# Short token tails of an expert layer: fp32 products of unsplit w2, four k at once in 32 array columns each

## The chip, the cores and the metric

The kernel runs on one core of a Trainium2 chip. The metric is device time in microseconds of one execution; the kernel before has a median of 837.87 us over three runs (837.8 to 838.12). The engines are TensorE (PE, with PEld for its weight loads), VectorE (DVE), ScalarE (ACT), GpSimd (POOL) and SyncE (SP), which here only issues DMA transfers. Each has an instruction queue of its own and runs it in order; semaphores tie them together.

## What is computed

Block-causal attention over 8 batches, 8 heads, 576 tokens and 64 dimensions makes 4608 rows of 512. Each row then goes to one of 16 experts (four groups of four), chosen by the largest logit, and its result is scaled by the two softmax weights:

```python
for g in range(G):
    mask_g = g_idx == g
    ...
    for e in range(Eg):
        mask_e = e_idx == e
        ...
        h = np.maximum(xg[mask_e] @ w1[g, e], 0.0)      # 512 -> 1024
        ye = h @ w2[g, e]                               # 1024 -> 512
        combined = g_w[mask_g][mask_e] * e_w[mask_e]
        out[tok_idx] = combined[:, None] * ye
```

## The kernel before

The first half of the span is attention, with the router among it. This case is about the second half, class `Moe`. Tokens are dealt into 15 **slots**, each one expert's tokens or part of them. The first ("e") has 512 tokens of the expert that is fullest after six batches; the others have fixed sizes, `CAPS` in units of 16 tokens, run in the order `EXEC`. In that order the slots have 528, 144, 448, 144, 448, 192, 416, 256, 320, 256, 320, 288, 272 and 128 tokens. In names a slot has its place in `CAPS`: `y6` belongs to the slot of 288 tokens, `h7` to the one of 272.

A slot's tokens are gathered (POOL, indirect DMA), transposed (`xt`, line 925) and put through two products. `g1` makes h = relu(x w1): the 1024 hidden units are eight k of 128, each four matmuls deep. `g2` makes y += h w2, with h as the stationary operand and 512 columns of w2 streaming. Precision comes from splitting: every fp32 operand becomes a high part in fp32r and the remainder (low), and three products (high high, low high, high low) stand for one fp32 product. Slots under 256 tokens leave w1 unsplit and multiply in fp32 (line 952), the others take the split (line 957). The relu of `g1` is made twice: ScalarE writes the high part (line 970), VectorE the low one (line 974).

Whole chunks of 128 tokens take three matmuls per k in `g2` (line 1002). What lies beyond them, when it is at most 64 tokens, is the **tail**. It puts its high and low part side by side into the stationary operand, `gap` columns apart (32 for up to 32 tokens, else 64), so that wh and wl each stream once: two matmuls per k (line 1007). The store (lines 1013 to 1035) then adds the two halves: a scaled copy of the low half on ScalarE (line 1020), and on VectorE the high half times the weight plus that copy (line 1021). Whole chunks are scaled by VectorE or ScalarE alone (lines 1027, 1029). GpSimd writes the rows out.

Weights come in **units** of 512 KB, eight per slot: w1 and w2 in turn, each for two k. SP loads a unit into one of four `raw` buffers; ScalarE casts it to wh, VectorE subtracts to wl, in two pieces each (lines 908, 909). There are `WBUFS` = 9 pairs of wh and wl. Unsplit w1 goes straight into a wh buffer (line 900).

The order of the work is written out beforehand. `plan` makes one list of steps: `g1` of k 0, the last `g2` of the slot before, `g1` of k 1, `g2` of k 0, and so on (a step is one k; two where the slot has 144 to 256 tokens, four where it has 128). It adds up TensorE's time by step and gives each weight piece a due time 9 us ahead of its first use (14 us for unsplit w1). `run` issues the steps; after each it issues transposes, loads (`pump`), the pieces that are due, at most two unless more are needed (`advance`), index loads (`getids`) and gathers, all into the queues of their engines. A piece may only be issued when the unit that had its buffer `WBUFS` units earlier has been used up (`limit`).

The router's logits (line 673) and the products of the attention weights with V (line 304) serve the prediction as measures. Both are fp32 and use a part of the array's columns:

```python
nc.tensor.matmul(ps[32 * c:32 * c + 32, z, 0:288], lhsT=self.w[p, c, :], rhs=xT[p, c, ks],     # L673, p: 64 rows
                 start=True, stop=True, tile_position=(64 * z, 32 * c))
...
    for a in range(2):
        nc.tensor.matmul(                                                                      # L304, 128 rows
            o[64 * a:64 * a + 64, hf, c0:c0 + BLK * (b1 - t)], lhsT=r["v"][:, a, j, :],
            rhs=pt[:, PTJ * j + t:PTJ * j + b1, a, :],
            start=x == 0, stop=x == len(pcs) - 1, tile_position=(0, 64 * a),
        )
```

A matmul in fp32 has two records in the trace, one in fp32r has one.

Of the kernel before, what the change touches and what calls it, by code (L numbers as in the profile page):

```python
# [8 lines left out]
F32 = mybir.dt.float32  # L9
# [3 lines left out]
AF = mybir.ActivationFunctionType  # L13
ALU = mybir.AluOpType
# [3 lines left out]
P = 128  # L18
D = 64
S = 576  # L20
# [372 lines left out]
CAPS = [33, 28, 28, 26, 20, 20, 18, 17, 16, 16, 12, 9, 9, 8]  # L393
EXEC = [0, 12, 1, 11, 2, 10, 3, 9, 4, 8, 5, 6, 7, 13]
EBAT = 6
WBUFS = 9
XBUFS = 5
PIECE = 760.0
LEAD = 9000.0
# [410 lines left out]
class Moe:  # L810
# [17 lines left out]
    def grow(self):  # L828
        t = self.at.vfix.tile([P, 6 * NT * D], F32R, tag="vb", name="hx")
        self.ring.append(t[:, 0:1152])  # L830

    def hbuf(self):
        self.nring += 1
        return self.ring[(self.nring - 1) % len(self.ring)]

    def slot(self, n, m, row, idx):
        T = UNIT * m
        nf, r = divmod(T, P)
        ch = [(c, P) for c in range(nf)] + ([(nf, r)] if r else [])
        nk = 1 if T > 256 else min(8, 1 << (512 // T).bit_length() - 1)  # L840
        return dict(n=n, m=m, T=T, gap=32 if r <= 32 else 64, nf=nf + (r > 64), tail=r if r <= 64 else 0, ch=ch, row=row, idx=idx, u={}, x={},
                    small=T < 256, nk=nk, nb=8 // nk)

    def index(self, s):
# [3 lines left out]
    def getids(self, s):  # L848
        if "ids" in s:
            return  # L850
        nc = self.nc
        s["st"] = nc.sync.value_load(s["row"][0:1, s["idx"], 1:2], min_val=0, max_val=PADS)
        s["ids"] = ids = self.ip.tile([P, 5, 2], I32, tag="ids", name=f"ids{s['n']}")
        table = lambda o, n: self.ro.tab[bass.ds(s["st"] + o, n), 0:2]
        full = s["T"] // P
        todo = [(ids[:, 0:full, :], table(0, full * P).rearrange("(c p) t -> p c t", p=P))] if full else []
        r = s["T"] % P
        if r:
            todo += [(ids[z:z + r, full, :], table(full * P, r)) for z in ((0, s["gap"]) if s["tail"] else (0,))]
        for o, i in todo:  # L860
            self.ro.after_writes(nc.sync.dma_start(o, i))

# [72 lines left out]
    def g1(self, s, b):  # L935
        nc = self.nc
        nk, T, r = s["nk"], s["T"], s["tail"]
        n = nk * T
        w0 = n if n <= 512 else n // 2
        ps = []  # L940
        for a in range(0, n, w0):
            p = self.at.psH(f"h{s['n']}_{b}_{a}")[:, 0:w0]
            ps.append((a, p))
            tw = min(T, w0)
            for k in range(w0 // tw):
                kg = b * nk + k
                w = self.w(s, 2 * (kg // 2))
                f = slice(kg % 2 * P, kg % 2 * P + P)
                o, t = p[:, k * tw:(k + 1) * tw], slice(a, a + tw)
                for dc in range(4):  # L950
                    if s["small"]:
                        nc.tensor.matmul(o, lhsT=w[0][:, dc, f].bitcast(F32), rhs=s["xh"][:, dc, t].bitcast(F32),  # L952
                                         start=dc == 0, stop=dc == 3)
                        continue
                    wh, wl = w
                    for x, (ww, rr) in enumerate(((wh, s["xh"]), (wh, s["xl"]), (wl, s["xh"]))):
                        nc.tensor.matmul(o, lhsT=ww[:, dc, f], rhs=rr[:, dc, t],  # L957
                                         start=dc == 0 and x == 0, stop=dc == 3 and x == 2)
        buf = self.hbuf()
        F = T - r  # L960
        pad = s["gap"] - r if r else 0
        L = T + pad
        g = buf[:, 0:nk * (L + T)].rearrange("p (k t) -> p k t", k=nk)
        hi, lt, lf = g[:, :, 0:T], g[:, :, L:L + r], g[:, :, L + r:L + T]
        if pad:
            nc.gpsimd.memset(g[:, :, T:L].bitcast(F32), 0.0)
        for a, p in ps:
            wa = min(T, w0)
            pv = p.rearrange("p (k t) -> p k t", t=wa)
            nc.scalar.activation(hi[:, :, a:a + wa], pv, AF.Relu)  # L970
            for t, t0, t1 in ((lf, 0, F), (lt, F, T)):
                q0, q1 = max(a, t0), min(a + wa, t1)
                if q0 < q1:
                    nc.vector.scalar_tensor_tensor(out=t[:, :, q0 - t0:q1 - t0], in0=pv[:, :, q0 - a:q1 - a], scalar=0.0,  # L974
                                                   in1=hi[:, :, q0:q1].bitcast(F32), op0=ALU.max, op1=ALU.subtract)
        s["h", b] = (hi, lf, g[:, :, F:L + r])

# [10 lines left out]
    def g2(self, s, b):  # L988
        nc = self.nc
        nk, T = s["nk"], s["T"]  # L990
        if b == 0:
            self.ytile(s)
        y, ks = s["y"], range(b * nk, (b + 1) * nk)

        for c in range(s["nf"]):
            n = s["ch"][c][1]
            r = slice(c * P, c * P + n)
            for k in ks:
                h, l = [t[:, k % nk, r] for t in s["h", b][0:2]]
                wh, wl = [w[:, k % 2, :] for w in self.w(s, 2 * (k // 2) + 1)]  # L1000
                for x, (hh, w) in enumerate(((h, wh), (h, wl), (l, wh))):
                    nc.tensor.matmul(y[c][0:n], lhsT=hh, rhs=w, start=k == 0 and x == 0, stop=k == 7 and x == 2)  # L1002
        if s["tail"]:
            n = s["gap"] + s["tail"]
            for k in ks:
                for x, w in enumerate(self.w(s, 2 * (k // 2) + 1)):
                    nc.tensor.matmul(y[s["nf"]][0:n], lhsT=s["h", b][2][:, k % nk, :], rhs=w[:, k % 2, :],  # L1007
                                     start=k == 0 and x == 0, stop=k == 7 and x == 1)
        if b == s["nb"] - 1:
            for c in range(len(s["ch"])):  # L1010
                self.store(s, c, c < s["nf"])

    def store(self, s, c, full):
        nc = self.nc
        ys = self.ro.rows.tile([P, 512], F32, tag="row", name=f"ys{s['n']}_{c}")
        n, y, cw = s["ch"][c][1], s["y"][c], s["ids"][:, c, 1:2].bitcast(F32)
        if not full:
            tmp = self.ro.rows.tile([P, 512], F32, tag="row", name=f"yt{s['n']}")
            z = s["gap"]
            nc.scalar.activation(tmp[0:n], y[z:z + n], AF.Copy, scale=cw[z:z + n])  # L1020
            nc.vector.scalar_tensor_tensor(out=ys[0:n], in0=y[0:n], scalar=cw[0:n], in1=tmp[0:n],
                                           op0=ALU.mult, op1=ALU.add)
        elif s.get("o") == len(self.slots) - 1:
            nc.scalar.activation(ys[0:n, 0:256], y[0:n, 0:256], AF.Copy, scale=cw[0:n])  # L1024
            nc.vector.tensor_scalar(out=ys[0:n, 256:512], in0=y[0:n, 256:512], scalar1=cw[0:n], scalar2=None, op0=ALU.mult)
        elif c % 2 == 0:
            nc.vector.tensor_scalar(out=ys[0:n], in0=y[0:n], scalar1=cw[0:n], scalar2=None, op0=ALU.mult)  # L1027
        else:
            nc.scalar.activation(ys[0:n], y[0:n], AF.Copy, scale=cw[0:n])
        nc.gpsimd.memset(self.ro.mark, 0.0)  # L1030
        i = nc.gpsimd.indirect_dma_start(  # L1031
            out=self.out, out_offset=bass.IndirectOffsetOnAxis(ap=s["ids"][0:n, c, 0:1], axis=0),
            in_=ys[0:n], in_offset=None, bounds_check=NTOK - 1, oob_is_err=False)
        self.ro.apart("out", i)

    def plan(self, slots):
        self.slots = slots
        seq = []
# [11 lines left out]
            prev = (s, "g2", s["nb"] - 1)  # L1050
        seq.append(prev)
        self.seq = seq
        self.units = [(s, u) for s in slots for u in range(8)]
        self.first, self.last = {}, {}
        self.tc0, t = [], 0.0
        self.begin = {}
        for n, (s, f, b) in enumerate(seq):
            self.tc0.append(t)
            nk = s["nk"]
            if f == "g1":  # L1060
                t += nk * 4 * s["T"] * (4 if s["small"] else 3) / 2.4
            else:
                t += nk * (3 * s["nf"] + 2 * (s["tail"] > 0)) * 216
            if (f, b) == ("g1", 0):
                self.begin[s["o"]] = n
                t += 430.0 * len(s["ch"])
            for k in range(b * nk, (b + 1) * nk):
                key = (s["o"], 2 * (k // 2) + (f == "g2"))
                self.first.setdefault(key, n)
                self.last[key] = n  # L1070
# [7 lines left out]
        for p in range(len(self.pieces) - 1, -1, -1):  # L1078
            ui, s, u, z = self.pieces[p]
# [54 lines left out]
    def run(self, hooks):  # L1134
        total = len(self.seq)
        for n, (s, f, b) in enumerate(self.seq):
# [3 lines left out]
            ready = n >= FREE  # L1140
# [11 lines left out]
            if ready:  # L1152
                for x in self.slots[1:]:
                    if "ids" not in x and self.tc0[self.begin[x["o"]]] - now < ILEAD:
                        self.getids(x)
            self.gathers(now, ready)
            yield

    def overflow(self, cnti, row):
# [19 lines left out]
def attention_moe(ctx, tc, q, k, v, w_group, w_expert, w1, w2, out, order=None, on_dve=None):  # L1179
    nc = tc.nc  # L1180
# [15 lines left out]
    with tc.manual_schedule(engines={ET.PE, ET.Activation, ET.DVE, ET.Pool, ET.SP}):  # L1196
        ro = Router(tc, ctx, consts, w_group, w_expert, tab, xd)
        moe = Moe(tc, ctx, consts, ro, w1, w2, out)
# [64 lines left out]
        for j in range(1, 3):  # L1263
            b("X", j)
        at.experts()
        b("G", 0)
        b("G", 1)
        for _ in run:
# [28 lines left out]
```

## Time and profile before

| | |
|---|---|
| median of the runs | 837.87 us |
| profiled execution: its time | 836.7 us |
| its span | 835.0 us |
| TensorE, VectorE, ScalarE, GpSimd busy | 95%, 63%, 60%, 32% |
| DMA in the whole span | 126.67 MB, 152 GB/s |
| raw weight loads | 96 of 512 KB |

The span is what the profiler saw between the first and the last instruction; the execution's own time is 1.7 us longer. Busy time is how long an engine had an instruction in it. Matmuls overlap, so a record is longer than the time until the next one starts; what a matmul costs is read from start to start, or from the chain. The chain is the work that ended last, followed back from the end: a line's share of it is what the span would lose without it, as long as nothing else becomes late.

### The profile page before, as it was taken

What the parts mean: (1) busy time and instruction counts of PE and PEld (TensorE: products, weight loads), DVE (VectorE), ACT (ScalarE), POOL (GpSimd) and SP (SyncE); (2) the same over time, 40 slices, a digit from 0 to 9 for tenths busy, and PEclk for the clock granted to TensorE, in tenths of its full rate; (3) what the DMA queues carried; (4) which work ended last, traced back from release to release, by engine and by line L of the source; (5) the groups of instructions that cost most, each with busy time, mean ns of one, the idle gap of its engine ahead of it and who ended that gap; (6) DMA issues with size and microseconds to landing.
All of it is one profiled execution on the core that took longest, in us unless ns stands there. A gap on an engine that the chain in (4) does not pass through costs nothing.

```text
span 835.0 us, 20289 instructions
## 1 busy us (share of the span) xinstructions
PE 795.5 (95%) x7649; PEld 649.7 (78%) x7649; DVE 529.3 (63%) x1102; ACT 504.6 (60%) x1273; POOL 265.9 (32%) x444
## 2 busy tenths in 40 slices
PE   8899999999999999879999999999999999999996
PEld 4677777777777777657888888888988989888885
DVE  4566989898989898668353544554444655655552
ACT  4899999999999998742342433433344445545541
POOL 3563344444444345443232211221221221131101
PEclk9899999999999999999999999999999999999999
DMA  7466473626363633641555736645544666575471
GB/s 153 114 185 181 109 157 78 155 71 150 83 152 78 145 84 90 198 153 36 177 166 162 236 117 205 201 133 192 197 145 148 203 207 191 179 237 177 151 236 39
DMA packets 182258, 126.67 MB, mean 152 GB/s; under 512 B 124902, under 2 KB 156214, under 8 KB 182160
## 3 DMA queue, kind: packets, MB, share of 16 engines
q1 hardware_dynamic: 173072, 100.73, 43.4%
q0 software_dynamic: 9088, 24.64, 8.6%
q8 instruction: 61, 1.00, 0.6%
q14 instruction: 37, 0.30, 0.1%
HBM read 100.88 MB, written 24.59 MB: 150 GB/s over the span
## 4 chain that ended last, share of the span: by engine, by line
PE 54%; DVE 1%; issue 0%; POOLq 0%; ACT 0%; ACTq 0%
PE y L1002 20%; PE h L957 19%; PE y L1007 5%; PE h L952 4%; PE ye L1002 2%; PE xp L925 2%; PE he L957 2%; POOLq L1293 0%; DVE gsc L712 0%; DVE gdd L710 0%; DVE goh L714 0%; DVE pre L742 0%; PE spill L612 0%; ACT ys L1024 0%; DVE sel L724 0%
## 5 line engine op out<-in xcount | busy, mean ns | idle before, releaser
L242 ACT ACTIVATE pb<-s,nm 128x512 f32<-128x512 f32 (+4 forms) x288 | 156.7, 556 | 31.3 <-DVE nm L230 26.7
L957 PE MATMUL h<-xt,wh 128*128 128x264 f32 (+6 forms) x704 | 155.3, 312 | 0.0
L909 DVE TENSOR_TENSOR wl<-raw,wh 128x512 fp32r<-128x512 f32 x192 | 123.4, 685 | 11.2 <-ACT wh L908 10.6
L230 DVE TENSOR_REDUCE nm<-s 128x2 f32<-128x1024 f32 (+4 forms) x160 | 122.9, 801 | 11.1 <-PE s L225 5.8
L957 PEld LDWEIGHTS h<-xt,wh 128*128 128x128 f32 x704 | 119.3, 188 | 9.1
L908 ACT CAST wh<-raw 128x512 fp32r<-128x512 f32 x192 | 108.8, 620 | 2.0 <-DMA raw<-in_moe_w_dram 1.7
L957 PE MATMUL h<-xt,wl 128*128 128x264 f32 (+6 forms) x352 | 109.3, 311 | 0.0
L1002 PE MATMUL y<-wh,hring 128*128 128x512 f32 x306 | 107.2, 401 | 0.0
L221 PE MATMUL s<-qk 64*128 64x512 f32 (+3 forms) x768 | 90.8, 351 | 12.6 <-ACT pb L242 7.3
L275 ACT COPY pt<-tp 128x1024 f32<-128x1024 f32 (+4 forms) x160 | 100.8, 747 | 0.5 <-PE tp L150 0.5
L1031 POOL DMA_INDIRECT out_dram<-ys,ids x40 | 41.2, 1029 | 183.4 <-DVE ys L1027 170.0
L970 ACT ACTIVATE hring<-h 128x288 fp32r<-128x288 f32 (+7 forms) x62 | 28.9, 466 | 114.0 <-PE h L957 55.3
L974 DVE SCALAR_TENSOR_TENSOR hring<-h,hring 128x32 fp32r<-128x32 f32 (+7 forms) x112 | 35.7, 357 | 97.5 <-ACT hring L970 89.2
L304 PE MATMUL o<-pt,vb 128*64 128x320 f32 (+4 forms) x896 | 93.9, 360 | 1.1 <-issue 1.1
L187 POOL CAST qk<-nf 128x640 fp32r<-128x640 f32 (+1 forms) x63 | 43.0, 694 | 150.8 <-ACT nf L275 140.4
L304 PEld LDWEIGHTS o<-pt,vb 128*64 128x64 f32 x896 | 59.6, 137 | 35.9 <-issue 5.1
L221 PEld LDWEIGHTS s<-qk 64*128 64x128 f32 x768 | 58.9, 190 | 24.8 <-issue 11.2
L872 POOL DMA_INDIRECT xg<-xd,ids x40 | 42.0, 1049 | 105.7 <-DMA ids<-tab 55.5
L150 PE MATMUL tp<-ident,pb 64*128 64x64 f32 x1600 | 65.5, 227 | 7.6 <-ACT pb L242 6.8
L150 PEld LDWEIGHTS tp<-ident,pb 64*128 64x128 f32 x1600 | 58.1, 141 | 14.3 <-ACT pb L242 8.0
L957 PEld LDWEIGHTS h<-xt,wl 128*128 128x128 f32 x352 | 66.2, 188 | 1.2
L1002 PEld LDWEIGHTS y<-wh,hring 128*128 128x128 f32 x306 | 57.6, 188 | 11.8
(236 smaller groups left out, 1396.5 us busy)
## 6 DMA issues: line engine op xcount, KB each, us to landing
raw<-in_moe_w_dram SPq DMA_DIRECT2D x96, 512.0 KB
natk<-in_k_dram SPq DMA_DIRECT2D x32, 256.0 KB
natq<-in_q_dram SPq DMA_DIRECT2D x32, 256.0 KB
vb<-in_v_dram SPq DMA_DIRECT2D x64, 128.0 KB
wh<-in_moe_w_dram SPq DMA_DIRECT2D x16, 512.0 KB
xd<-xns SPq DMA_DIRECT2D x14, 512.0 KB
tab<-fill POOLq DMA_DIRECT2D x10, 512.0 KB
rawe<-in_moe_w_dram SPq DMA_DIRECT2D x8, 512.0 KB
```

Source lines behind the costliest of these rows:

```text
L150: self.nc.tensor.transpose(out=out[:, z], in_=src[r], identity=self.c["ident"][r, r])
L187: (eng or self.side(("h", n))).tensor_copy(r["qk"][:, 0, o], r["nf"][:, o])
L221: nc.tensor.matmul(st[:, z, :], lhsT=t[p, hq, S + P * u:S + P * u + P], rhs=t[p, hk, 0:w], start=x == 0, stop=False)
L230: self.nc.vector.tensor_reduce(out=o, in_=r["s", u], op=ALU.max, axis=ax, negate=True)
L242: nc.scalar.activation(reg, src, AF.Exp, bias=r["nm"][:, t:t + 1], accum_out=self.sms[b][:, pr, z, u:u + 1])
L275: return self.nc.scalar.copy(dst, src)
L304: nc.tensor.matmul(o[64 * a:64 * a + 64, hf, c0:c0 + BLK * (b1 - t)], lhsT=r["v"][:, a, j, :], rhs=pt[:, PTJ * j + t:PTJ * j + b1, a, :], ...
L872: self.nc.gpsimd.indirect_dma_start(out=x[0:n], out_offset=None, in_=src, in_offset=bass.IndirectOffsetOnAxis(ap=s["ids"][0:n, c, 0:1], ax ...
L908: nc.scalar.copy(h[:, sl], s["raw", u][:, sl])
L909: nc.vector.tensor_tensor(out=l[:, sl], in0=s["raw", u][:, sl], in1=h[:, sl].bitcast(F32), op=ALU.subtract)
L957: nc.tensor.matmul(o, lhsT=ww[:, dc, f], rhs=rr[:, dc, t], start=dc == 0 and x == 0, stop=dc == 3 and x == 2)
L1002: nc.tensor.matmul(y[c][0:n], lhsT=hh, rhs=w, start=k == 0 and x == 0, stop=k == 7 and x == 2)
```

## The change

Tails of 16 or 32 tokens (`quad`; the slots of 528, 416, 288, 272, 144 and 144 tokens) take another way. Their relu is written once, in fp32 and without a split, into a buffer `th`. After every fourth k, `tails` issues one fp32 matmul for each of those four k, with unsplit w2 as the streaming operand. The four stand in 32 columns of the array each, and so in 32 partitions of one PSUM bank each; the second four of a slot add to them. Unsplit w2 is read once more for that, into `rawq`: two buffers of four k, loaded two visits ahead (`qload`). The store adds four parts instead of two. `WBUFS` falls from 9 to 8, which makes the room. The index loads put the tail's indices at four places instead of two. Tails of 64 tokens, whole chunks and the steps stay as they were.

```diff
-WBUFS = 9
+WBUFS = 8
...
+    def grow_raw(self):
+        t = self.at.xpool.tile([P, 4 * S], F32, tag="xT", name="rawq")
+        self.rawq = [x[:, 0:2048].rearrange("p (k f) -> p k f", k=4) for x in (t, self.ro.late.tile([P, 2048], F32, name="rawq2"))]
+        self.th = [x.rearrange("p (k r) -> p k r", k=8) for x in (t[:, 2048:], self.ro.late.tile([P, 256], F32, name="th"))]
...
-            todo += [(ids[z:z + r, full, :], table(full * P, r)) for z in ((0, s["gap"]) if s["tail"] else (0,))]
+            todo += [(ids[z:z + r, full, :], table(full * P, r)) for z in range(0, P if s["tail"] else 1, s["gap"])]
...
+        if s["quad"]:
+            g = buf[:, 0:nk * 2 * F].rearrange("p (k t) -> p k t", k=nk)
+            hi, lf, tl = g[:, :, 0:F], g[:, :, F:], self.th[s["qn"] % 2][:, b * nk:b * nk + nk, 0:r]
+            for a, p in ps:
...
+                nc.scalar.activation(hi[:, :, a:q1], pv[:, :, 0:q1 - a], AF.Relu)
+                nc.vector.scalar_tensor_tensor(out=lf[:, :, a:q1], in0=pv[:, :, 0:q1 - a], scalar=0.0,
+                                               in1=hi[:, :, a:q1].bitcast(F32), op0=ALU.max, op1=ALU.subtract)
+                if a + wa > F:
+                    nc.vector.tensor_scalar(out=tl, in0=pv[:, :, F - a:], scalar1=0.0, scalar2=None, op0=ALU.max)
...
-        if s["tail"]:
+        if s["quad"]:
+            if ks[-1] % 4 == 3:
+                self.tails(s, ks[-1] // 4)
+        elif s["tail"]:
...
+    def tails(self, s, half):
+
+        y, r = s["y"][s["nf"]], s["tail"]
+        for k in range(4):
+            q = 32 * k
+            self.nc.tensor.matmul(y[q:q + r], lhsT=self.th[s["qn"] % 2][:, 4 * half + k, 0:r], rhs=self.rawq[self.nvis % 2][:, k, :],
+                                  start=half == 0, stop=half == 1, tile_position=(0, q))
+        self.nvis += 1
+
+    def qload(self, n, ready):
+        if self.nqld < min(len(self.quads), self.nvis + 2) and ready:
+            s, half = self.quads[self.nqld]
+            self.index(s)
+            for j in range(2):
+                src, c = self.wsrc(s, 4 * half + 2 * j + 1)
+                self.nc.sync.dma_start(self.rawq[self.nqld % 2][:, 2 * j:2 * j + 2, :], src)
+            self.nqld += 1
...
-            z = s["gap"]
+            z = P - s["gap"]
             nc.scalar.activation(tmp[0:n], y[z:z + n], AF.Copy, scale=cw[z:z + n])
-            nc.vector.scalar_tensor_tensor(out=ys[0:n], in0=y[0:n], scalar=cw[0:n], in1=tmp[0:n],
-                                           op0=ALU.mult, op1=ALU.add)
+            while z:
+                z -= s["gap"]
+                src, tmp = tmp, tmp if z else ys
+                nc.vector.scalar_tensor_tensor(out=tmp[0:n], in0=y[z:z + n], scalar=cw[z:z + n], in1=src[0:n],
+                                               op0=ALU.mult, op1=ALU.add)
...
-                t += nk * (3 * s["nf"] + 2 * (s["tail"] > 0)) * 216
+                t += nk * (3 * s["nf"] + (1.2 if s["quad"] else 2 * (s["tail"] > 0))) * 216
...
             self.gathers(now, ready)
+            self.qload(n, ready)
```

The order of the instructions changes at two places that matter here. The first is TensorE's last `g2` step of the slot with 288 tokens (`y6`: two whole chunks in one tile, `y6_2`: its tail of 32 tokens). Before:

```order
L1002 MATMUL y6_11211<-wh6_7_11312,hx_7080 128x512
L1002 MATMUL y6_11211<-wl6_7_11313,hx_7080 128x512
L1002 MATMUL y6_11211<-wh6_7_11312,hx_7080 128x512 x2
L1002 MATMUL y6_11211<-wl6_7_11313,hx_7080 128x512
L1002 MATMUL y6_11211<-wh6_7_11312,hx_7080 128x512
L1007 MATMUL y6_2_11212<-wh6_7_11312,hx_7080 64x512
L1007 MATMUL y6_2_11212<-wl6_7_11313,hx_7080 64x512
L957 MATMUL h7_1_0_11505<-xt7_11376,wh7_0_11328 128x272 x2
```

After, where line 1021 is what line 1002 was, and 963 what 957 was:

```order
L1021 MATMUL y6_11206<-wh6_7_11301,hx_7080 128x512
L1021 MATMUL y6_11206<-wl6_7_11302,hx_7080 128x512
L1021 MATMUL y6_11206<-wh6_7_11301,hx_7080 128x512 x2
L1021 MATMUL y6_11206<-wl6_7_11302,hx_7080 128x512
L1021 MATMUL y6_11206<-wh6_7_11301,hx_7080 128x512
L1040 MATMUL y6_2_11207<-rawq2_7257,rawq_7256 32x512 x4
L963 MATMUL h7_1_0_11510<-xt7_11367,wh7_0_11319 128x272 x2
```

The two tail matmuls are gone from this step, as from the seven before it; four fp32 matmuls stand in their place here and after the fourth k.

The second is VectorE at the end of the same slot, between the low halves of h for k 0 and k 1 of the next slot (`h7_0`, `h7_1`; `wl7_3` and `wl7_4` are casts, `ys6_0` the store of chunk 0). Before:

```order
L974 SCALAR_TENSOR_TENSOR hring_7009<-h7_0_0_11446,hring_7009 128x256
L974 SCALAR_TENSOR_TENSOR hring_7009<-h7_0_0_11446,hring_7009 128x16
L909 TENSOR_TENSOR wl7_3_11464<-raw7_3_11326,wh7_3_11463 128x512
L1027 TENSOR_SCALAR ys6_0_11477<-y6_11211,ids6_10668 128x512
L1021 SCALAR_TENSOR_TENSOR ys6_2_11489<-y6_2_11212,ids6_10668,yt6_11490 32x512
L909 TENSOR_TENSOR wl7_3_11464<-raw7_3_11326,wh7_3_11463 128x512
L909 TENSOR_TENSOR wl7_4_11502<-raw7_4_11350,wh7_4_11501 128x512
L974 SCALAR_TENSOR_TENSOR hring_7009<-h7_1_0_11505,hring_7009 128x256
L974 SCALAR_TENSOR_TENSOR hring_7009<-h7_1_0_11505,hring_7009 128x16
```

After (915 was 909, 1070 was 1027, 1064 was 1021, 974 is the low half):

```order
L974 SCALAR_TENSOR_TENSOR hring_7009<-h7_0_0_11433,hring_7009 128x256
L977 TENSOR_SCALAR th_7258<-h7_0_0_11433 128x16
L915 TENSOR_TENSOR wl7_3_11450<-raw7_3_11307,wh7_3_11449 128x512 x2
L1070 TENSOR_SCALAR ys6_0_11469<-y6_11206,ids6_10668 128x512
L1064 SCALAR_TENSOR_TENSOR yt6_11482<-y6_2_11207,ids6_10668,yt6_11482 32x512 x2
L1064 SCALAR_TENSOR_TENSOR ys6_2_11481<-y6_2_11207,ids6_10668,yt6_11482 32x512
L915 TENSOR_TENSOR wl7_4_11492<-raw7_4_11325,wh7_4_11491 128x512 x2
L974 SCALAR_TENSOR_TENSOR hring_7009<-h7_1_0_11510,hring_7009 128x256
L977 TENSOR_SCALAR th_7258<-h7_1_0_11510 128x16
```

The store of the tail has three instructions instead of one, the second cast of `wl7_3` has moved ahead of the stores, and four casts instead of three stand between the two low halves.

## Rows read from the trace of the kernel before

**Rows 1.** Busy us, share and instructions of each engine, the page's part 1.
```profile
PE 795.5 (95%) x7649; PEld 649.7 (78%) x7649; DVE 529.3 (63%) x1102; ACT 504.6 (60%) x1273; POOL 265.9 (32%) x444
```

**Rows 2.** The chain that ended last, the page's part 4: by engine, by line.
```profile
PE 54%; DVE 1%; issue 0%; POOLq 0%; ACT 0%; ACTq 0%
PE y L1002 20%; PE h L957 19%; PE y L1007 5%; PE h L952 4%; PE ye L1002 2%; PE xp L925 2%; PE he L957 2%; POOLq L1293 0%; DVE gsc L712 0%; DVE gdd L710 0%; DVE goh L714 0%; DVE pre L742 0%; PE spill L612 0%; ACT ys L1024 0%; DVE sel L724 0%
```

**Rows 3.** Stretches of 50 us: length, busy us, clock, DMA share, GB/s.
```profile
450.00:500.00 50.00, 50.00 (x287) 42.35 (x286) 23.32 (x48) 19.71 (x39) 12.86 (x24) 1.00 0.59 189
...
750.00:800.00 50.00, 50.00 (x297) 43.20 (x296) 31.71 (x69) 27.57 (x56) 9.52 (x20) 1.00 0.57 184
```

**Rows 4.** Line 1007: count, ns min/median/max, first and last start, forms.
```profile
L1007 PE MATMUL y<-wh,hring x59: 389/392/399, 432.1 to 818.1; 128*128 128x512 f32 x26, 128*48 128x512 f32 x23, 128*64 128x512 f32 x10
...
L1007 PE MATMUL y<-wh,hx x29: 388/393/398, 426.0 to 808.8; 128*128 128x512 f32 x14, 128*48 128x512 f32 x9, 128*64 128x512 f32 x6
```

**Rows 5.** The chain in order of time, 780 us on: start, us, line.
```profile
788.75 0.46 PE y L1007 x2
789.21 1.52 PE h L957 x12
790.72 1.45 PE y L1002 x6
...
813.27 3.57 PE h L952 x32
```

**Rows 6.** TensorE, 70 to 76 us: start, us, line, shapes, count.
```profile
71.81 0.71 PE L673 MATMUL lg<-xT,wcat 64*32 64x288 f32 x16
72.45 2.92 PE L304 MATMUL o<-pt,vb 128*64 128x256 f32 x28
75.31 0.27 PE L168 MATMUL o<-ident,natk 64*128 64x64 f32 x2
```

**Rows 7.** Short stretches, columns as in rows 3.
```profile
464.00:480.00 16.00, 16.00 (x102) 13.59 (x101) 8.10 (x16) 7.37 (x14) 5.90 (x13) 1.00 0.80 261
...
788.00:792.00 4.00, 4.00 (x24) 3.35 (x23) 2.53 (x6) 2.53 (x5) 1.75 (x3) 1.00 0.49 166
...
800.00:804.00 4.00, 4.00 (x27) 3.51 (x27) 2.74 (x6) 1.56 (x4) 0.11 (x1) 1.00 1.01 358
```

**Rows 8.** Waits of ScalarE, 430 to 835 us: total us, times, longest.
```profile
ACT wh L908 <- DMA raw<-in_moe_w_dram: 1.7, 2, 1.0
```

**Rows 9.** SP's DMA issues in order of time, 520 to 835 us.
```profile
799.22 10.43 SPq L900 DMA_DIRECT2D wh<-in_moe_w_dram  x4
```

**Rows 10.** VectorE in order of time, 787 to 795 us.
```profile
787.87 0.51 DVE L974 SCALAR_TENSOR_TENSOR hring<-h,hring 128x256 fp32r<-128x256 f32 x2 [1.72 <-ACT hring L970]
788.38 0.69 DVE L909 TENSOR_TENSOR wl<-raw,wh 128x512 fp32r<-128x512 f32 x1
788.98 0.75 DVE L1027 TENSOR_SCALAR ys<-y,ids 128x512 f32<-128x512 f32 x1
791.19 0.74 DVE L1021 SCALAR_TENSOR_TENSOR ys<-y,ids,yt 32x512 f32<-32x512 f32 x1 [1.46 <-ACT yt L1020]
791.86 1.27 DVE L909 TENSOR_TENSOR wl<-raw,wh 128x512 fp32r<-128x512 f32 x2
793.06 0.49 DVE L974 SCALAR_TENSOR_TENSOR hring<-h,hring 128x256 fp32r<-128x256 f32 x2
```

**Rows 11.** TensorE in order of time, 786 to 800 us.
```profile
787.19 0.39 PE L1002 MATMUL y<-wh,hx 128*128 128x512 f32 x1
...
788.58 0.39 PE L1007 MATMUL y<-wh,hx 128*64 128x512 f32 x1
...
793.99 0.40 PE L1002 MATMUL y<-wh,hring 128*128 128x512 f32 x1
...
794.45 0.63 PE L1002 MATMUL y<-wh,hring 128*128 128x512 f32 x2
```

More of the change, by code (lines that the diff above doesn't have):

```diff
@@ L839, in slot @@
         ch = [(c, P) for c in range(nf)] + ([(nf, r)] if r else [])
+        quad = 0 < r <= 32
         nk = 1 if T > 256 else min(8, 1 << (512 // T).bit_length() - 1)
-        return dict(n=n, m=m, T=T, gap=32 if r <= 32 else 64, nf=nf + (r > 64), tail=r if r <= 64 else 0, ch=ch, row=row, idx=idx, u={}, x={},
+        return dict(n=n, m=m, T=T, gap=32 if quad else 64, quad=quad, nf=nf + (r > 64), tail=r if r <= 64 else 0, ch=ch, row=row, idx=idx, u={}, x={},
                     small=T < 256, nk=nk, nb=8 // nk)
@@ L960, in g1 @@
         F = T - r
+        if s["quad"]:
+            g = buf[:, 0:nk * 2 * F].rearrange("p (k t) -> p k t", k=nk)
+            hi, lf, tl = g[:, :, 0:F], g[:, :, F:], self.th[s["qn"] % 2][:, b * nk:b * nk + nk, 0:r]
+            for a, p in ps:
+                wa = min(T, w0)
+                pv, q1 = p.rearrange("p (k t) -> p k t", t=wa), min(a + wa, F)
+                nc.scalar.activation(hi[:, :, a:q1], pv[:, :, 0:q1 - a], AF.Relu)
[3 more added lines that the diff above has]
+                    nc.vector.tensor_scalar(out=tl, in0=pv[:, :, F - a:], scalar1=0.0, scalar2=None, op0=ALU.max)
+            s["h", b] = (hi, lf)
+            return
         pad = s["gap"] - r if r else 0
@@ L1052, in plan @@
         self.seq = seq
+        self.quads = []
+        for s, f, b in seq:
+            k = (b + 1) * s["nk"]
+            if s["quad"] and f == "g2" and k % 4 == 0:
+                self.quads.append((s, k // 4 - 1))
+                s["qn"] = (len(self.quads) - 1) // 2
+        self.nvis = self.nqld = 0
         self.units = [(s, u) for s in slots for u in range(8)]
@@ L1265, in attention_moe @@
         at.experts()
+        moe.grow_raw()
         b("G", 0)
```

## The prediction

> **What bounds the kernel now.** [...] First the busy times of the page: TensorE has 795.5 of the 835.0 us of the span, VectorE and ScalarE about 60% each [rows 1]. Then the chain that ended last: the two matmuls of the experts, line 957 and line 1002, are 39% of the span, line 1007, which the change replaces, another 5%, and nothing but TensorE has more than 1% [rows 2]. [...] So in the expert stage each us taken from TensorE is a us off the end, until something else becomes late. [...]
>
> **What the change removes.** The tail of a slot (the tokens beyond whole chunks of 128) is multiplied in line 1007, two matmuls (wh and wl) for each of 8 k. 88 pairs are in the trace [rows 4]: 11 slots with a tail. The records with 48 stationary columns (16 tokens, gap 32; 32 pairs) and with 64 (32 tokens; 16 pairs) are the ones that go: six slots, 528, 416, 288, 272, 144 and 144 tokens, 48 pairs, 96 matmuls. The five slots with 64 tokens over stay. A pair has 0.46 us of the chain [rows 5], so 48 x 0.46 = 22.1 us leave TensorE.
>
> **What it adds on TensorE.** Twelve visits (two per slot), each of four fp32 matmuls of 512 columns, one in each group of 32 array columns. No row shows this shape, so I bound it. An fp32 matmul over the whole array: 16 of 128 columns (32 records, two each) take 3.57 us [rows 5], 0.223 us each or 1.74 ns a column, so 512 columns take 0.89 us. If the four run side by side a visit costs that and some edge; if they run one behind the other, 3.57 us. Two groups of rows decide. The router's logits (line 673) are eight fp32 matmuls of 288 columns, four column groups of 32 times two halves of the rows; they start at 71.81 and the next group starts at 72.45 [rows 6]. One alone would take 288 x 1.74 = 0.50 us, eight in turn 4.0: they run side by side, with 0.14 us of edge, which holds the change of tile shape at both ends. The products P times V (line 304) are nearer in the other respect: full 128 rows, two column groups of 64. Per head their seven pieces have 256, 128, 320, 320, 320, 192 and 64 columns, 1600; two heads in turn would take 3200 x 1.74 = 5.6 us, and they take 72.45 to 75.31, 2.86 us [rows 6]. So full-height column groups overlap, and four of them do at half height. I take side by side: 0.89 + 0.14 = 1.03 us, and by the logits' own record (0.71 rather than 0.64 us) 1.10; in between, 1.07. Twelve visits are 12.8 us. The ends I keep: 0.89 us without any edge (10.7 us in all), and 1.21 us (14.5 us) where both edges are fully exposed: an fp32r matmul of 512 columns has a record of 0.39 us [rows 4] and its successor starts 0.23 us later (half a pair), which leaves 0.16 us per edge.
>
> [...]
>
> TensorE net: -22.1 + 12.8 = -9.3 us.
>
> **What it adds elsewhere, and what hides it.** (a) Unsplit w2 is read again for these slots: 24 loads of 512 KB, 12.6 MB. A pair is issued when the visit two before it has been issued, behind the raw load of the same step; the nearest visit comes eight steps of TensorE later, each at least the 1.4 us of one full chunk [rows 5], so 11 us or more. On SP the pair waits for the matmuls of that visit, and the raw loads queued behind it wait for casts of later steps anyway, so I cost the wait at nothing. The bandwidth is not free: the DMA engines are at share 0.80 in 464 to 480 us, where two of the pairs will fall, and 1.01 with 358 GB/s in 800 to 804, beside 0.49 in 788 to 792 [rows 7]. ScalarE waited for a raw weight only twice, 1.7 us together [rows 8]. A pair of loads is 1.05 MB, 2.9 us at 358 GB/s; the planner casts with 9 us of lead, so I take 0 and keep 2.9 us for the upper end. (b) WBUFS 9 to 8: the order moves a few casts and direct loads of w1 by one or two steps. The last direct loads were issued from 799.22 over 10.43 us [rows 9], four steps before their matmuls; one step later they still have some 8 us: 0. (c) ScalarE's relu has fewer columns, GpSimd loses its memsets, VectorE's tail piece is one instruction as before: 0. (d) Two more small index loads per slot are 0.6 us each on SP, far ahead of their gathers: 0. (e) The store of such a tail has three VectorE instructions instead of one, 0.74 us each [rows 10], and the tail's PSUM bank is held as much longer. This is the one place where a cover goes. Where the next slot's steps are long (five of the six) I cost it at nothing: a low half of h is due only two steps after its relu. At the end of the slot with 288 tokens, before one of 272, steps are short. Before: after the low half of h for k 0 (787.87 to 788.38) VectorE does one cast, the store of chunk 0, the tail 2.2 us after that store's start, two casts, and the low half for k 1 at 793.06 [rows 10], which the third matmul of the step needs at 794.45 [rows 11]: 1.0 us of slack behind its first piece (ends about 793.5). After: the order has both casts ahead of the store, then three tail instructions, two casts, and the low half. From 788.4: two casts 1.3, the store at 789.7, the tail 2.2 later at 791.9, three times 0.7, two casts 1.3, low half 0.4: ready at 795.7. TensorE gets there hardly later than before: from 787.19, 1.39 of full chunk [rows 11], 1.07 for the visit, then 1.52, 1.45, 1.52 [rows 5] and 0.46 for two matmuls: 794.6. So it waits about 1.1 us, and with the cast backlog behind it 0.3 more at the next step: 1.4 us. Its ends are 0 (if the scheduler's gaps close) and 2 us.
>
> **Sum.** -22.1 + 12.8 + 1.4 = -7.9 us. The profiled execution took 836.7 us (835.0 of span and 1.7 around it), so 828.8; the runs shown have a median of 837.87, 1.2 above it, and there I forecast 837.87 - 7.9 = 830.0 us.
>
> **Rivals.** [...] With two at a time, the only full-height case shown, a visit is 1.92 us, twelve are 23.0, and the time is 840.2.
> [...]
> (2) The second reading of w2 comes into the way: each of the three pairs that fall into the full stretches (two in 464 to 480, one near 792 to 808) pushes raw or direct weights back by its 2.9 us, ScalarE waits in order and relu behind it, and TensorE idles: 8.7 us, which eats the gain: 838.7 us. For it speaks the share of 1.01 [rows 7]; against it that a raw weight is loaded four units ahead, and that ScalarE waited 1.7 us in all.
> (3) The change doesn't do what it says: it does, the order shows one group of four in the place of eight.
>
> **How the numbers follow.** Forecast 0.83, rival 1 0.09 (of which two at a time 0.04), rival 2 in full 0.08. The forecast's ends: -22.1 + 10.7 + 0 = -11.4, 826.5 us; and -22.1 + 14.5 + 2 + 2.9 = -2.7, 835.2 us. Inside it I leave out the outermost corners: 826.3 to 834.5 (the lower end a little under, as a pair is 0.465 rather than 0.46). Outside lie the rivals, some 0.17 to 0.2. About 0.2% (1.7 us) is what a measurement of this kernel can tell from no change. Faster by more than that: the forecast and part of rival 2, 0.85; the same: most of rival 2, 0.07; slower: rival 1, 0.08.
>
> **What would show it.** [...] In the chain line 1007 should fall from 5% to the five slots that keep it (40 pairs, 2%), with 12.8 us at the new line. TensorE's only new idle time should be 1 to 2 us where the slot of 288 tokens ends, put down to VectorE's low half of h; idle time put down to DMA, in ScalarE's casts or TensorE's weights, is rival 2. My forecast is wrong if the saving is under 3 us or over 12.

## The result

The changed kernel takes 827.95 us (median of four runs, 827.56 to 830.06), beside 838.0 for the kernel before: a ratio of 0.9881, 95% interval 0.986 to 0.9902, faster by about 1.2%. In a second set of runs, on another chip, where the kernel before took 831.11, it took 824.71: 0.9909 (0.9886 to 0.9932). A ratio is estimated from all runs of a set; it need not be the quotient of the two medians (0.9923 there). The forecast was 830.0 us, 7.9 less than before.

### The profile page after: what moved, and what is told of

The parts are those of the page before. It is cut to its first block, busy times and chain, and to the rows that moved or that the text cites. A ratio compares the mean times of both kernels' runs of the same rounds, so it can differ in the third digit from the quotient of the medians.

```text
span 828.3 us, 20396 instructions
## 1 busy us (share of the span) xinstructions
PE 787.7 (95%) x7649; PEld 639.4 (77%) x7649; DVE 537.7 (65%) x1114; ACT 503.5 (61%) x1273; POOL 267.2 (32%) x420
## 4 chain that ended last, share of the span: by engine, by line
PE 52%; DVE 1%; issue 1%; ACT 0%; POOLq 0%; DVEq 0%; ACTq 0%
PE y L1021 19%; PE h L963 19%; PE h L958 4%; PE ye L1021 2%; PE y L1029 2%; PE xp L931 2%; PE he L963 2%; PE y L1040 1%; DVE wl L915 0%; POOLq L1345 0%; DVE gsc L712 0%; DVE gdd L710 0%; DVE yt L1064 0%; DVE goh L714 0%; DVE ys L1070 0%
## 5 line engine op out<-in xcount | busy, mean ns | idle before, releaser
L1074 POOL DMA_INDIRECT out_dram<-ys,ids x40 | 44.7, 1117 | 200.4 <-DVE ys L1070 182.8
L878 POOL DMA_INDIRECT xg<-xd,ids x40 | 41.6, 1040 | 120.3 <-DMA ids<-tab 75.2
L1021 PE MATMUL y<-wl,hring 128*128 128x512 f32 x153 | 60.6, 396 | 0.0
L242 ACT ACTIVATION_READ_ACCUMULATOR pb<-s,nm 128x1 f32 x288 | 59.9, 208 | 0.0
```

Source lines behind the costliest of these rows:

```text
L242: nc.scalar.activation(reg, src, AF.Exp, bias=r["nm"][:, t:t + 1], accum_out=self.sms[b][:, pr, z, u:u + 1])
L1074: i = nc.gpsimd.indirect_dma_start(out=self.out, out_offset=bass.IndirectOffsetOnAxis(ap=s["ids"][0:n, c, 0:1], axis=0), in_=ys[0:n], in_o ...
```

## The profile after

The profiled execution took 830.06 us with a span of 828.3. First the page's busy times and its chain by line (lines 1021 and 963 are the old 1002 and 957, line 1029 is what is left of 1007, line 1040 is the new tails):

```profile
PE 787.7 (95%) x7649; PEld 639.4 (77%) x7649; DVE 537.7 (65%) x1114; ACT 503.5 (61%) x1273; POOL 267.2 (32%) x420
...
PE y L1021 19%; PE h L963 19%; PE h L958 4%; PE ye L1021 2%; PE y L1029 2%; PE xp L931 2%; PE he L963 2%; PE y L1040 1%; DVE wl L915 0%; POOLq L1345 0%; DVE gsc L712 0%; DVE gdd L710 0%; DVE yt L1064 0%; DVE goh L714 0%; DVE ys L1070 0%
```

Beside [rows 2] the tails went from 5% to 2 + 1%. The same two stretches as [rows 3]: the DMA share rose from 0.59 and 0.57, and TensorE is no longer full in the second.

```profile
450.00:500.00 50.00, 50.00 (x296) 41.45 (x295) 26.21 (x52) 19.60 (x40) 11.91 (x17) 1.00 0.81 259
750.00:800.00 50.00, 49.17 (x303) 41.01 (x302) 33.43 (x73) 26.61 (x54) 7.87 (x13) 1.00 0.74 243
```

The missing 0.83 us is the only wait of TensorE in the expert stage, in its list of waits (total, times, longest):

```profile
PE y L1021 <- DVE hring L974: 0.8, 1, 0.8
```

One visit in TensorE's order of time (start, duration, line, stationary shape, moving shape, count):

```profile
443.28 0.39 PE L1021 MATMUL y<-wl,hx 128*128 128x512 f32 x1
443.51 0.40 PE L1021 MATMUL y<-wh,hx 128*128 128x512 f32 x1
443.84 1.05 PE L1040 MATMUL y<-rawq 128*16 128x512 f32 x8
444.82 0.51 PE L963 MATMUL h<-xt,wh 128*128 128x264 f32 x2
445.17 0.29 PE L963 MATMUL h<-xt,wl 128*128 128x264 f32 x1
```

Four fp32 matmuls (two records each) take 0.98 us from their start to the next group's. But the price doesn't end there. The y matmul ahead is followed after 0.33 us (443.51 to 443.84), its neighbours after 0.23; and the pair of h matmuls behind takes 0.35 (444.82 to 445.17), where such a pair takes 0.24 elsewhere. The visit costs 0.98 + 0.10 + 0.11 = 1.19 us here; read the same way, the twelve cost 1.12 to 1.20 us, 14.1 together. Part of a visit's edges lies on its neighbours. TensorE's weight loads around the same visit:

```profile
443.84 0.13 PEld L1040 LDWEIGHTS y<-rawq 128*16 128x16 f32 x8 [0.37 <-issue]
444.82 0.30 PEld L963 LDWEIGHTS h<-xt,wh 128*128 128x128 f32 x2 [0.85 <-issue]
```

All eight loads of the visit (two to a matmul) are done 0.13 us after its first matmul starts; the four run side by side. And at both changes of tile shape the load begins only with its matmul (443.84 and 444.82).

The stage from the first expert matmul of h to the last of y is the measure for what follows. Of the kernel before:

```profile
414.58 0.41 PE L957 MATMUL h<-xt,wh 128*128 128x264 f32 x2
...
827.48 0.39 PE L1002 MATMUL y<-wh,hring 128*128 128x512 f32 x1
```

and of the changed one:

```profile
415.22 0.41 PE L963 MATMUL h<-xt,wh 128*128 128x264 f32 x2
...
820.78 0.39 PE L1021 MATMUL y<-wh,hring 128*128 128x512 f32 x1
```

412.90 us and 405.56: 7.34 less. The terms, each read from starts in the traces: 48 pairs out (22.2), twelve visits in (14.1), and 1.1 us by which the stall delays the matmuls (0.83 of it idle; see the last part): -7.0 us. The other 0.3 us is made of differences under 0.06 us each, and no run shows their cause. Of the 10.0 us by which the first runs differ, 2.7 are not in this stage of the two traces.

## The experiments

Every kernel gets the length of that stage ("stage", from its own trace) beside its time and that of the kernel before in the same set of runs. There are three sets, each on a chip of its own (before: 831.98, 831.11 and 836.92 us). "TensorE waits" is TensorE's idle time in the stage.

| kernel | us | before | ratio (95%) | stage | TensorE waits |
|---|---|---|---|---|---|
| before, again | 835.89 | 836.92 | 0.9985 (0.997 to 0.9999) | 412.87 | 0 |
| changed, again | 824.71 | 831.11 | 0.9909 (0.9886 to 0.9932) | 405.60 | 0.8 |
| second reading alone | 831.13 | 831.98 | 0.9982 (0.997 to 0.9993) | 412.90 | 0 |
| no second reading | 824.01 | 831.98 | 0.9901 (0.9884 to 0.9918) | 405.61 | 0.8 |
| one column group | 853.03 | 831.98 | 1.0249 (1.0233 to 1.0264) | 435.43 | 0 |
| two column groups | 838.68 | 836.92 | 1.002 (1.0007 to 1.0032) | 414.97 | 0 |
| each visit twice | 832.74 | 831.98 | 1.0012 (1.0001 to 1.0023) | 415.14 | 0 |
| one full tile | 826.16 | 836.92 | 0.9871 (0.9845 to 0.9898) | 402.38 | 0.9 |
| store one step later | 832.13 | 831.11 | 1.0 (0.9983 to 1.0016) | 411.90 | 6.6 |
| one visit per slot | 821.76 | 831.11 | 0.9885 (0.9862 to 0.9908) | 402.90 | 0 |
| both of the last two | 830.19 | 831.11 | 0.9983 (0.9964 to 1.0001) | 411.10 | 5.9 |

**Both kernels again.**

> The changed kernel again, on the chip and beside the runs of the kernel before that the next three are compared with. In the first traces the stage from the first expert matmul to the last (412.90 us before, 405.56 after) explains 7.3 us of the runs' 10.0. Theory (the other 2.7 are what the stage ahead of the experts happens to take from chip to chip and run to run): 7 to 9 us under the kernel before, and again 405.6 us for the expert stage. Rival (the change shortens something else by 2.7 us): 10 us under it on this chip too.

> The kernel before again, for its trace on a second chip, where its runs took 831 to 832 us in place of 838. Theory (the two chips differ ahead of the experts, not in them): first expert matmul at about 409 to 411 us in place of 414.6, and 412.9 us from there to the last one. Rival (the second chip is faster in the expert stage as well): under 411 us there.

The stage repeats to 0.04 us, while its start moves: 414.58 and 417.49 in the two traces of before, 415.22 and 410.17 in the two of after, 408.3 to 413.7 in the experiments. The start of the second trace of before was expected at 409 to 411 us; that trace came from the third chip, where the kernel takes 836.92 us. The saving of the second set, 0.9% of 831.11 or 7.6 us (5.7 to 9.5 by its interval; 6.4 between the medians), agrees with the stage's 7.3. So the 10.0 us of the first set are probably not the change's alone. An unchanged copy gave a ratio of 0.9985 with an interval that leaves 1 out: differences of 0.15% between medians here are no effect.

**The second reading.** In the one kernel the tails are multiplied as before and the visits are only counted, so that the loads are made; in the other the loads stop after two visits:

```
-            for j in range(2):
+            for j in range(2 if self.nqld < 2 else 0):
```

> The tails are multiplied as before (wh and wl, eight k), but the second reading of w2 (24 loads of 512 KB), WBUFS 8 and the two more index loads per slot are there; nothing reads what the second reading brings. Theory (these parts cost nothing): 838.0 us, within 0.8 of the kernel before, and no idle time of TensorE in the expert stage. Rival A (the reading gets in the way of raw or direct weights): 840 to 846.7, with idle time put down to DMA or to ScalarE's casts. Rival B: the saving of the changed kernel's runs (10.0 us) is 2.7 larger than what its trace shows between the first and the last expert matmul (7.3); if the layout or the loads gave these 2.7, this kernel shows 835.3.

> The changed kernel, with the second reading of w2 only for the first two visits; later visits multiply what lies there, so ten of the twelve visits compute with the wrong weights, with the same instructions. Theory (the reading is covered): 828.0 us, within 0.8 of the changed kernel; ScalarE's 4.6 us of waits for raw weights fall to about the 1.7 of before. Rival (the reading delays weights and eats part of the gain): faster by 1 to 8.7 us, 819.3 to 827.

The reading alone:

```profile
409.27 0.41 PE L963 MATMUL h<-xt,wh 128*128 128x264 f32 x2
...
822.17 0.39 PE L1021 MATMUL y<-wh,hring 128*128 128x512 f32 x1
```

412.90 us, as before to the hundredth; without it 405.61, as with it. It costs nothing, with eight weight buffers in place of nine. It does disturb one engine: ScalarE's waits on the raw weights grew from 1.7 us [rows 8] to, in the changed kernel,

```profile
ACT wh L914 <- DMA raw<-in_moe_w_dram: 4.6, 2, 2.7
```

and TensorE waited for none of it. They are 3.3 us with the reading alone and 2.2 without it.

**Column groups.** One group, or two (`q = 32 * (k % 2)`), in the place of four:

```
-            q = 32 * k
+            q = 0
```

> The changed kernel with the four tail matmuls of a visit in one and the same group of 32 array columns, summed in one PSUM range; the store adds that range four times, so the tails come out four times too large. Theory (four different column groups run side by side, one group takes them in turn): a visit grows from 0.98 us to 4 x 0.89 + 0.1 = 3.66, twelve by 32.2 us: 860.2, or 859.4 if the 0.8 us stall disappears behind them. Rival (it is the small stationary tile that makes the visit cheap, not the four groups): under 835.

> The changed kernel with the four tail matmuls of a visit in two groups of array columns, two behind each other in each group; the store adds the two sums twice, so the tails come out twice too large. Theory (a group takes its matmuls in turn, 0.87 us each, and different groups run side by side): a visit grows by 0.87, twelve by 10.4 us; the 0.83 us stall goes: expert stage 415.1 us, about 9.6 us over the changed kernel. Rival (two full-height groups share something that four share as well, so that two by two is no worse): about 405.6 us.

The same visit with one group:

```profile
436.93 3.61 PE L1040 MATMUL y<-rawq 128*16 128x512 f32 x8
440.47 0.51 PE L963 MATMUL h<-xt,wh 128*128 128x264 f32 x2
```

3.54 us in place of 0.98. Without side-by-side execution the change would have been 2.5% slower than the kernel before; four groups are worth 29.9 us of the stage. The theory's 31.4 to 32.2 was too much: it counted a visit of the changed kernel at 0.98 us, without the edges on its neighbours.

**Edges.** Each visit twice (`for x in range(2)` around the four), and one matmul over the whole array in the place of four tiles:

```
-            self.nc.tensor.matmul(y[q:q + r], lhsT=self.th[...][:, 4 * half + k, 0:r], rhs=..., tile_position=(0, q))
+            self.nc.tensor.matmul(y[0:P], lhsT=self.c["ident"], rhs=...)
```

> The changed kernel with each visit's four matmuls issued twice in a row, so the tails come out twice as large. It takes the edges of a visit apart from its body. Theory (body 0.89 us, 512 columns of 1.74 ns; of the 1.18 us that a visit costs in the trace, 0.98 to the next start and 0.10 each on the matmuls before and behind, 0.29 is edge): the second four add 0.89 each, 10.7 us: 838.7. Rival A (no edge, all is body): 12 x 1.18 = 14.2 more, 842.2. [...]

> The changed kernel with one fp32 matmul of 512 columns over the whole array (128 by 128, the identity as weights) in the place of each visit's four, so the tails are not multiplied at all: it takes the change of tile shape away from the edges. Theory (the 0.31 us of edges belong to the change of tile): a visit costs about 0.87 us, 12 x 0.31 = 3.7 us less: expert stage 401.9 us. Rival (the edges belong to the step from fp32r to fp32 and back): 405.6 us as with four tiles. Between them lies a share of each.

Read from the starts as above (the interval ahead, the visit, the first interval behind, less what the two intervals take elsewhere), the mean over the visits is 1.18 us for the changed kernel, 2.02 for two in turn per group, 2.03 for the doubled visit, 3.73 for four in turn, and 0.86 for the full tile. The first four fit 0.32 + 0.85 x (matmuls in turn per group), with one, two or four groups and with four or eight matmuls alike, so the edge is not a stagger of the four. The doubled visits make the stage 9.6 us longer, where 10.7 were expected: twelve times 0.86, and 0.9 of the stall is gone. Full tile, one visit:

```profile
441.98 0.40 PE L1021 MATMUL y<-wh,hx 128*128 128x512 f32 x1
442.21 1.02 PE L1039 MATMUL y<-rawq,ident 128*128 128x512 f32 x2
442.67 0.81 PE L963 MATMUL h<-xt,wh 128*128 128x264 f32 x2
443.31 0.28 PE L963 MATMUL h<-xt,wl 128*128 128x264 f32 x1
```

The matmul ahead is followed after 0.23 us again, and from 442.21 to the third h matmul it takes 1.10 us, 0.24 of them the pair's own: 0.86, the body alone. So the edges' 0.32 us come with the change of tile shape, and none of them with fp32. (The stage is 0.5 us longer than the theory's 401.9, mostly by delays of 0.1 and 0.3 us around 648 and 780 us.) The weight loads go with that:

```profile
441.98 0.42 PEld L1039 LDWEIGHTS y<-rawq,ident 128*128 128x128 f32 x2
```

A full tile's first load begins with the matmul ahead, 0.23 us before its own; across a change of shape, above, it begins with its own. What else makes up the 0.32 us stays open.

**The stall, and a better kernel.** The tail's store one step later; and both visits of a slot at its end, the edit shown:

```
-            if ks[-1] % 4 == 3:
-                self.tails(s, ks[-1] // 4)
+            if ks[-1] == 7:
+                self.tails(s, 0)
+                self.tails(s, 1)
```

> The changed kernel, with the store of such a tail (one ScalarE and three VectorE instructions) issued one step later, behind the next slot's relu pieces. Theory (the 0.83 us stall at the end of the 288-token slot is VectorE's queue: three tail instructions ahead of the low half of h): no stall, expert stage 404.7 us, 0.8 us under the changed kernel. Rival A (casts set it): the stall stays. Rival B (a later step's low half or cast is late instead): the stall moves on, 405.6 us.

> The changed kernel, with the two visits of a slot issued one behind the other at the end of the slot: six visits of eight matmuls instead of twelve of four. Theory (a visit has a body of 0.87 us and 0.31 us of edges, from the run with doubled visits): six edges less, 1.9 us: expert stage 403.7 us. Rival A (both pairs of loads of the next slot now start only at the end of this one, and come late): TensorE waits for DMA, slower. Rival B (no gain, the edges belong to the change of PSUM bank or weights, not to the visit): 405.6 us.

> Both of the two before in one kernel. Theory (they concern different waits and add): expert stage 402.9 us, 2.7 us under the changed kernel, 10 us under the kernel before. Rival (the later visit puts the later store into the way of the next slot): no better than the better of the two.

The late store failed in a way that none of the three theories had. TensorE's waits with it:

```profile
PE y L1029 <- DVE ys L1067: 3.4, 2, 1.7
PE y L1021 <- DVE ys L1067: 2.5, 1, 2.5
PE y L1021 <- DVE hx L974: 0.7, 1, 0.7
```

Line 1067 is the last of the three additions. The tail's PSUM bank goes to a chunk or the tail of the next slot (line 1029 is a tail of 64 tokens), whose first matmuls come within one step; three times TensorE now waits for the store to free it. The last row is rival B: the stall of the 288-token slot moved on by one step and shrank by only 0.2 us (0.83 to 0.66).

One visit per slot is 2.7 us shorter in its stage than the changed kernel. One of its visits:

```profile
460.72 1.05 PE L1041 MATMUL y<-rawq 128*16 128x512 f32 x8
461.59 1.04 PE L1041 MATMUL y<-rawq,rawq 128*16 128x512 f32 x8
462.56 2.23 PE L958 MATMUL h<-xt,wh 128*128 128x144 f32 x16
```

The second four start 0.87 us after the first, without an edge. Six edges of 0.32 make 1.9 us; the other 0.8 is the stall, which is gone but for 0.2 us: the slot's end is now 0.9 us longer on TensorE, and VectorE is almost in time. That the next slot's loads start later did no harm: no wait for DMA. With 821.76 us beside 824.71 in the same set it has the lowest median and stage of the kernels that compute everything; the intervals of the two ratios overlap, so its lead rests on the trace. Both edits together take 8.2 us more in the stage than one visit per slot. The same three waits make 6.5 of it by the starts (5.9 idle). Another 1.6 come behind the longest wait (2.5 us, to 651.86), where the granted clock was 0.51 and then 0.64 in stretches of 2 us, and matmuls of 512 columns started every 0.43 us instead of 0.23:

```profile
652.00:654.00 2.00, 2.00 (x6) 1.52 (x7) 2.00 (x4) 0.00 (x0) 2.00 (x1) 0.51 1.02 369
654.00:656.00 2.00, 2.00 (x12) 1.90 (x11) 0.12 (x1) 0.00 (x0) 0.35 (x2) 0.64 0.86 296
```

The late store alone has a wait as long there (2.5 us, to 653.03) and kept a clock of 1.00; no run shows what decides. Without the 1.6 us both edits would have about 409.5 us, an estimate, 2.4 below the late store: the edges and the stall are saved in this kernel too, and the PSUM waits cost more.

## Why the prediction was right

- **TensorE bounds the stage**: yes, as its 50.00 of 50.00 us in both stretches of [rows 3] have it. What left TensorE left the end; the one new wait is in the trace.
- **Removed, 22.1 us**: right (22.2 by the starts).
- **Added, 12.8 us**: the step that was mis-sized. Side by side was right, and the body nearly so (0.89 forecast, 0.85 measured). The edge was taken from the logits, 0.14 us, with 1.07 for the visit; it is 0.32, and the visit 1.18, 14.1 us in all, near the upper end of 14.5. The text looked for the edge between a visit's start and the next group's, where only 0.1 us of it stands; the rest is on the matmuls ahead and behind. The logits have a change of tile on both sides too, but their successor is another narrow tile, not a full one. The full-tile run has no edge (0.86 us per visit, 0.32 less), so the price is that of the change of shape at both ends, and the forecast should have stood nearer to its upper end, 1.21 us with both edges exposed. What makes an edge cost that, no run shows.
- **The stall, 1.4 us**: right in place and cause; the first wait had the right size, the second did not come. VectorE at the end of the 288-token slot, beside [rows 10]:

```profile
782.44 0.74 DVE L1070 TENSOR_SCALAR ys<-y,ids 128x512 f32<-128x512 f32 x1
784.65 1.52 DVE L1064 SCALAR_TENSOR_TENSOR yt<-y,ids,yt 32x512 f32<-32x512 f32 x2 [1.47 <-ACT ys L1072]
786.20 0.74 DVE L1064 SCALAR_TENSOR_TENSOR ys<-y,ids,yt 32x512 f32<-32x512 f32 x1
786.87 1.29 DVE L915 TENSOR_TENSOR wl<-raw,wh 128x512 fp32r<-128x512 f32 x2
788.09 0.41 DVE L974 SCALAR_TENSOR_TENSOR hring<-h,hring 128x256 fp32r<-128x256 f32 x1
```

and TensorE beside it:

```profile
780.10 0.39 PE L1021 MATMUL y<-wh,hx 128*128 128x512 f32 x1
...
787.32 0.40 PE L1021 MATMUL y<-wl,hring 128*128 128x512 f32 x1
788.55 0.73 PE L1021 MATMUL y<-wh,hring 128*128 128x512 f32 x2 [0.83 <-DVE hring L974]
789.12 0.39 PE L1021 MATMUL y<-wl,hring 128*128 128x512 f32 x1
```

  The low half came 5.65 us after the start of chunk 0's store (782.44 to 788.09), where the forecast had 5.6. Without the wait TensorE's third matmul would have started 0.23 us after the second, at 787.55, 7.45 us after the slot's last full chunks began (780.10), where the forecast had 7.4. It started at 788.55, 1.0 us later, and the next two intervals are 0.1 us longer than elsewhere (0.57 in place of 0.47): 1.1 us, as forecast. The list's 0.83 us is less because the record of the second matmul runs on to 787.72. The further 0.3 us at the next step did not come: the list has one wait.
- **Costs set at nothing** (second reading, eight buffers, index loads, relu): right, shown for the first three by the run with the reading alone, whose stage is as long as before. Rival 2 falls. One reading on the way was wrong: the 1.45 us of [rows 5] are six matmuls, two full chunks and not one. The bound of 11 us that was built on it held: from a visit to the second one after it the least is 18.1 us (467.87 to 485.97).
- **Rival 1**, the four one behind the other, falls too: one group costs 3.73 us a visit, two 2.02, near the forecast's 3.57 for four in turn (without an edge) and 1.92 for two at a time. In the changed kernel the loads of the four full-height tiles are done 0.13 us after the first of their matmuls starts, and the visit takes 1.18 us.
- **The sum**: -7.9 forecast, -7.3 in the stage: 1.3 us too little for the visits, 0.3 too much for the stall, 0.4 in small differences. On the forecast's base of 837.87 the stage's 7.3 alone would have given 830.5. In the first runs the time came out 2 us under the forecast, for a reason that no step names. The stage ahead of the experts varies by more than that; in the profiled execution of after the granted clock fell there:

```profile
340.00:360.00 20.00, 14.13 (x175) 10.80 (x171) 12.63 (x43) 10.17 (x23) 9.00 (x18) 0.90 0.51 165
360.00:380.00 20.00, 16.66 (x138) 12.30 (x139) 13.55 (x27) 8.86 (x18) 5.62 (x9) 0.85 0.49 159
```

  In before's trace:

```profile
340.00:360.00 20.00, 14.19 (x213) 10.92 (x211) 12.42 (x43) 12.25 (x28) 9.02 (x17) 1.00 0.57 185
360.00:380.00 20.00, 17.23 (x141) 12.56 (x142) 14.61 (x34) 8.71 (x18) 6.26 (x11) 0.91 0.52 165
```

  The granted clock was 0.90 and 0.85 beside 1.00 and 0.91, though TensorE was busy nearly as long in the first stretch in both (14.13 and 14.19 of 20 us). That execution, 830.06 us, was the slowest of its four, so the fall cannot be what put the others 2 us under the forecast; it shows what varies there. In the second set the time of the kernel before goes with the clock too: from 829.29 us at a mean granted clock of 0.997 to 836.13 at 0.985. What made the unprofiled runs of the first set differ by 10.0 us stays open.

## What to carry to other kernels

An edge between tile shapes is paid on the neighbours too (0.10 and 0.11 us of the 1.19 in the visit shown): measure it as the change of the interval from the instruction before to the one after, and group work of one shape so that it is paid once per slot, not twice (six edges of 0.32 us here). A store that can wait for its data may still not wait: look who gets its PSUM bank next (5.9 us of TensorE's waits with the late store). To compare kernels by less than 0.5%, compare the one stage that the edit touches in both traces; it repeated to 0.04 us here, where medians of an identical kernel differed by 1 us.

## What the hardware showed that was not expected

Full-height tiles of 32 columns with four different stationary and four different moving operands ran fully side by side: four in four groups 1.18 us, four in one group 3.73. A switch from full fp32r tiles to narrow fp32 tiles and back cost 0.32 us, and the weight load at each switch began only with its matmul; from full fp32r to full fp32 and back cost nothing (0.86 us, the body alone), and on the way there the load began 0.23 us ahead. After one wait of 2.5 us the granted clock was 0.51 and then 0.64 in two stretches of 2 us, and after another as long it stayed at 1.00.
